# The first batch's pooled remainder in the prologue, and a fourth buffer for raw weights

## The chip, the cores and the metric

One core of one Trainium2 chip runs the whole kernel. The metric is the device time of one execution in microseconds (us). TensorE does the matmuls, VectorE and ScalarE the element work, GpSimd (POOL) additions and indirect DMAs, SyncE (SP) issues the plain DMAs.

## The reference, cut to what matters

Three layers follow one another. The first is attention over 4 batches, 8 heads, 576 positions, 64 wide, and its output is the sum of two attentions: one over sequences pooled by 4 (144 positions, repeated 4 times), one over a local band. The other two are layers of 8 experts, each token going to one.

```python
q_d = q.reshape(B, H, Sd, factor, D).mean(axis=3)      # k_d, v_d alike; Sd = 144
out_up = np.repeat(sm_attn(q_d, k_d, v_d), factor, axis=2)
mask = np.abs(pos[:, None] - pos[None, :]) < factor
scores = np.where(mask, scale * np.matmul(q, k.transpose(0, 1, 3, 2)), -1e9)
...
return out_up + np.matmul(softmax(scores), v)
# _moe_ref, N = 2304, D = 512, E = 8, F = 1024 (the second layer has no output gate)
e_idx = np.argmax(x @ w_gate, axis=1)
h = np.maximum(x[mask] @ w1[e], 0.0)
out[mask] = gate_w[mask, None] * eom[mask, e, None] * (h @ w2[e])
```

## The kernel before, in words

**Pooled attention.** A batch has 144 pooled queries for each head. Heads go in 4 pairs; class `Pooled(b, c)` does the first 128 queries of pair c = 0 to 3, and with c = 4 the *remainder*, the last 16 queries' part of all pairs at once (32 rows a pair, so that four column tiles of TensorE hold four pairs). Its steps: `scores` (matmuls into a bank of PSUM), `smax` (maximum and difference on VectorE), `exps` (ScalarE), `flip` (three transposes on TensorE), `evac` (copy on ScalarE), `pvs` (product with the pooled values `vpd`), `norm`. Pooled sums come from POOL for the most part (`sums_k`, `sums_q`, `sums_v`). In the first batch the pairs 0 and 1 don't wait for pooled queries: their scores are four matmuls, one for each of the four positions that are pooled, that add up in PSUM (`QPE = 2`). For the remainder of that batch (L517 to L528) this makes four matmuls for each of the pairs 0 and 1, one pair after the other, and one each for the pairs 2 and 3; a matmul of f32 is two instructions in the trace.

**Local attention.** `Local(i)` does one of 20 tiles (5 a batch): `scores`, softmax, `flip`, `pvs` (which also adds the pooled output `od` through a 0/1 matrix `rep`), `xevac` (copies rows to SBUF and stores 58 or fewer rows with each of two DMAs, L690), transposes, and the logits of the first expert layer.

**Order.** The prologue is a list of names, `PRO` (L72): `F` sums of keys, `s`, `m`, `f` the start, middle and finish of a pooled pair, `V` and `A` sums, `l...` loads. Then 23 steps follow; each runs `ORDER` over up to three local tiles in different stages and the pooled work set for that step (`pooled_at`). The remainder of the first batch is set for step 0 (`REM0`), so its scores are in step 0 and its transposition and product in step 1. From this order, which gives priorities, a planner in the compiler makes the order on each engine; it goes by its own estimate of when inputs are there, and an instruction of lower priority can pass one that isn't ready. On the chip each engine then works in that fixed order. All pooled work and transposes in attention share a pool of two PSUM buffers (`psx`).

**Experts.** The first layer's tokens are routed as attention goes (`route`: `pick`, `count`, `place`, `spread`, `put`; `put` is a matmul into a list in PSUM). After step 18 the fullest expert so far is picked (`snap`), its first 256 rows are gathered by indirect DMA (`fetch`, L1156), and weights are loaded ahead (`prime`). Weights come in 128 chunks c of 512 KB: `load_next` loads a chunk into one of `NRAW` buffers, `split_next` casts it to its high part `wh` (ScalarE, L1127) and takes the remainder `wl` (VectorE, L1135), which frees the buffer. A job's rows are transposed (`xpose`, L1206) and cast to `xh` (ScalarE, L1216) and `xl` (VectorE, L1219). `hide` makes one of eight hidden blocks with 12 matmuls, two blocks a chunk; chunks 4 to 7 are the second matrix.

**Edges written by hand.** The cast of chunk 0 is put behind the last transposed copy of attention, and the cast of chunk `PINX` behind the casts of the first job's rows:

```python
if c in (0, PINX):
    for p in after if c else front:
        tc.add_manual_dep(i.ins, p.ins.name, ...)   # "the rows go ahead of weights"
i = nc.vector.tensor_tensor(lo, raw, hi.bitcast(F32), op=ALU.subtract)
if c == PINX:
    tc.add_manual_dep(i.ins, placed[0].ins.name, ...)  # "the places of the last tokens go ahead"
```

`PINX` is 4 with three raw buffers, so the chunks 0 to 2 are loaded ahead, chunk 3 is the first to wait for a buffer, and the edge holds chunk 4.

Of the kernel before, what the change touches and what calls it, by code (L numbers as in the profile page):

```python
# [9 lines left out]
F32 = mybir.dt.float32  # L10
# [11 lines left out]
NP = H // 2  # L22
SD = S // 4
# [5 lines left out]
DM = 512  # L29
# [5 lines left out]
MAGIC = 12582912.0  # L35
NOV = 32
NWB = 9
NRAW = 3

CAPS = (  # L40
    (512, 384, 352, 320, 304, 288, 272, 256),
# [6 lines left out]
NWE = 3  # L48
POOLSPLIT = 0
POOLHI = 0  # L50
REM0 = 0
PUTN = 2
PB = (3, 2, 3, 2, 1)
PUTS = 15
# [9 lines left out]
XA = 99  # L64
STEPF = {}
RLATE = 0
PINX = 4
QPE = 2
KPOOL = 0
Q1POOL = 0  # L70
S1 = "pppp"
PRO = "F0 s0 V0 s1 F2 s2 s3 zq m1 Ls m0 m2 f0 f1 lqk lvr f2 m3 V1 A0 lcs rep A2 f3 Le lvw zp lw1"  # L72
ORDER = "R As Ae q0f Cf Xt Cp p0s Xl Xs An p0e q1f p1s q0p Cx D p1e K q1p S"

C_ID = 0
# [105 lines left out]
def moe_pair_kernel(  # L181
# [17 lines left out]
    nc = tc.nc  # L199
# [194 lines left out]
    def attention(actx, early, early_x, front):  # L394
# [11 lines left out]
        kpd = [side[i].tile([128, 2, NP, SD], F32, name=f"kpd{i}") for i in range(2)]  # L406
# [3 lines left out]
        rep = sb1.tile([128, NTP + NP, 128], F32R, name="rep")  # L410
        qd = {}
# [83 lines left out]
        class Pooled:  # L495
# [6 lines left out]
            def scores(self):  # L502
                b, c = self.b, self.c
                ps = psx.tile([128, 512], F32, tag="m", name="s")
                sv = ps[:, 0:2 * SD].rearrange("p (s k) -> p s k", s=2)
                if c < NP:
                    if b == 0 and c < QPE:
                        src = qt[b % 3][:, c, 0:512].rearrange("p (t r) -> p t r", r=4)
                        for r in range(4):
                            nc.tensor.matmul(  # L510
                                sv, lhsT=src[:, :, r], rhs=kpd[b % 2][:, :, c, :],
                                start=(r == 0), stop=(r == 3),
                            )
                    else:
                        nc.tensor.matmul(sv, lhsT=qd[b][:, c, 0:128], rhs=kpd[b % 2][:, :, c, :])
                else:
                    for a in range(NP):  # L517
                        if b == 0 and a < QPE:
                            src = qt[b % 3][:, a, S - 128:S].rearrange("p (t r) -> p t r", r=4)
                            ls = [src[:, :, r] for r in range(4)]  # L520
                        else:
                            ls = [qd[b][:, a, SD - 32:SD]]
                        for i, l in enumerate(ls):
                            nc.tensor.matmul(
                                sv[32 * a:32 * a + 32], lhsT=l,
                                rhs=kpd[b % 2][:, :, a, :], tile_position=(0, 32 * a),
                                start=(i == 0), stop=(i == len(ls) - 1), skip_group_check=True,
                            )  # L528
                self.sv = sv

            def smax(self):
# [189 lines left out]
        pooled_at = {}  # L721
        for b in range(B):
            s0 = NTP * (b - 1) + 2
            for c in range(NP + 1):
                if b or c == NP:
                    pooled_at.setdefault(s0 + c // 2 if b else REM0, []).append(Pooled(b, c))
        groups = GROUPS
        lgs_of = {}
        for g0, gn in groups:
# [29 lines left out]
        for i in range(3):  # L759
            t = sb3.tile([128, 3, 128], F32, tag="p", name="p")  # L760
            nc.sync.dma_start(t, crep[:, 3 * i:3 * i + 3])
            stg.append(t)
        c0 = [Pooled(0, c) for c in range(NP)]

        def start(c):
            c0[c].scores()
# [41 lines left out]
            "A0": lambda: sums1(0),  # L808
            "A2": lambda: sums1(2),
        }  # L810
        for c in range(NP):
            pro.update({
                f"s{c}": lambda c=c: start(c), f"m{c}": lambda c=c: middle(c), f"f{c}": lambda c=c: finish(c),
            })
        for o in PRO.split():
            pro[o]()

        for s in range(-1, NL + 3):
# [6 lines left out]
            if 0 <= s:  # L825
                b, r = s // NTP + 1, s % NTP
# [143 lines left out]
    def experts():  # L970
        pl = {}
# [4 lines left out]
        def pool(nm, bufs=1, **kw):  # L976
            pl[nm] = ctx.enter_context(tc.tile_pool(name=nm, bufs=bufs, reuse_waits="tile", **kw))

        def pools_early():
            pool("raw", NRAW)  # L980
            pool("xr", 5)
            pool("x0")
            pool("w0", NWE)
            pool("h0")
            pool("sm", 2)
# [109 lines left out]
        def load_next():  # L1095
            c = nxt[0]
            if c >= len(stream) or c - nxt[1] >= NRAW:
                return
# [4 lines left out]
            if j == 0:  # L1103
                M.e_sp[r] = M.eid(r)
            raws[c] = pl["raw"].tile([128, 1024], F32, tag="raw", name="raw", bufs=NRAW)
            load_w(raws[c], M, M.e_sp[r], j, M.by_rows[r])
# [43 lines left out]
        def prime():  # L1150
            for _ in range(NRAW):
                load_next()
# [13 lines left out]
        def fetch(job, fresh=None):  # L1166
# [10 lines left out]
            seen = tiles // NTP * S + tiles % NTP * 2 * GQ  # L1177
            x = []
            for k, mm in job.slots:
                xr = pl["xr"].tile([128, DM], F32, tag="xr", name="xr", bufs=5)  # L1180
                gather(M, xr, ri, k, mm, seen if job is M0.jobs[0] else NT)
                x.append(xr)
            job.x = x
# [121 lines left out]
        def overflow_slot(M, m, nov, i):  # L1305
# [39 lines left out]
            nc.vector.scalar_tensor_tensor(  # L1345
                ri[:, 0, 1:2], rf[:, 0, 0:1], -1.0, bg, op0=ALU.add, op1=ALU.add
            )
            xr = pl["xr"].tile([128, DM], F32, tag="xr", name="xr", bufs=5)
            gather(M, xr, ri, 0, 128)
            pt = psx.tile([128, 4, 128], F32, tag="m", name="t")  # L1350
            for d in range(4):
# [5 lines left out]
            for j in range(8):  # L1357
                raw = pl["raw"].tile([128, 1024], F32, tag="raw", name="raw", bufs=NRAW)
                load_w(raw, M, e, j)
                rv = raw.rearrange("p (a w) -> p a w", w=256 if j < 4 else 128)  # L1360
                if j < 4:
                    for f2 in range(2):
                        ph = psx.tile([128, 512], F32, tag="m", name="ph")
                        for d in range(4):
                            nc.tensor.matmul(
                                ph[:, 0:128], lhsT=rv[:, d, 128 * f2:128 * f2 + 128], rhs=xt[:, d],
                                start=(d == 0), stop=(d == 3),
                            )
                        nc.scalar.activation(ht[:, 2 * j + f2], ph[:, 0:128], func=AF.Relu)
                else:  # L1370
                    for f in range(8):
                        nc.tensor.matmul(
                            py[:, 128 * (j - 4):128 * (j - 4) + 128], lhsT=ht[:, f], rhs=rv[:, f],
                            start=(f == 0), stop=(f == 7), skip_group_check=True,
# [259 lines left out]
```

## Time and profile before

| what | value |
|---|---|
| median of 3 runs | 747.93 us (747.17 to 748.26) |
| profiled execution | 742.5 us, its span 740.7 us |
| TensorE busy | 697.6 us, 94% of the span |
| VectorE, ScalarE, POOL busy | 446.3, 343.5, 184.6 us |
| mean granted TensorE clock | 0.972 |

A profile lists the instructions of one execution by engine. PE is TensorE's matmuls, PEld its weight loads, DVE VectorE, ACT ScalarE. `out<-in` are the program's tile names. Behind an instruction, in brackets, is the idle time of its engine just before it and what ended that. The granted clock is a share of 2.4 GHz; 0.50 is 1.2 GHz. Times count from the start of the span.

### The profile page before, as it was taken

The numbers are of one execution on the slowest core, as the hardware profiler recorded it, in microseconds if no ns is written. First come the engines' busy times: TensorE is split into PE (matmuls) and PEld (weight loads), VectorE is DVE, ScalarE is ACT, GpSimd is POOL, SyncE is SP. The second block draws the span as 40 slices with busy tenths as digits, with TensorE's granted clock in tenths as the row PEclk, the third lists the DMA queues.
The fourth block names the chain that finished last, engine by engine and source line by source line (L and its number), as shares of the span: only waits on it lengthen the run. The fifth ranks groups of instructions, "written<-read, shape, count | busy, mean of one in ns | idle before, by whom it ended". The sixth has DMA issues, their size and how long they took to land. (4 is left out here: it accounts for less than half of the span.)

```text
span 740.7 us, 15853 instructions
## 1 busy us (share of the span) xinstructions
PE 697.6 (94%) x6048; PEld 637.4 (86%) x6048; DVE 446.3 (60%) x1160; ACT 343.5 (46%) x634; POOL 184.6 (25%) x227
## 2 busy tenths in 40 slices
PE   8799899976989999999999999989999999999993
PEld 5468677765989999999999999878999999999992
DVE  7486979785667656575766776645444444555520
ACT  4055657584255353545454554155335354554620
POOL 5994720010131203121130130142013030321211
PEclk9699999996999999999999999999999999999998
DMA  9945553143176435445555461366435354565500
GB/s 354 420 140 210 184 196 132 55 156 131 58 247 207 160 121 183 140 161 179 173 176 168 141 221 59 110 213 217 128 111 182 126 186 141 176 193 178 163 21 16
DMA packets 52990, 120.99 MB, mean 163 GB/s; under 512 B 4800, under 2 KB 26176, under 8 KB 51884
## 3 DMA queue, kind: packets, MB, share of 16 engines
q1 hardware_dynamic: 45772, 99.19, 39.9%
q0 software_dynamic: 7136, 20.72, 8.2%
q8 instruction: 50, 0.82, 0.5%
q14 instruction: 32, 0.26, 0.1%
HBM read 101.01 MB, written 20.71 MB: 164 GB/s over the span
## 5 line engine op out<-in xcount | busy, mean ns | idle before, releaser
L1135 DVE TENSOR_TENSOR wl<-raw,wh 128x1024 fp32r<-128x1024 f32 x128 | 156.2, 1224 | 115.7 <-ACT wh L1127 115.4
L1127 ACT CAST wh<-raw 128x1024 fp32r<-128x1024 f32 x128 | 133.2, 1048 | 197.7 <-PE py L1295 113.3
L1294 PE MATMUL ph<-xh,wh 128*128 128x256 f32 (+8 forms) x576 | 172.3, 307 | 6.6 <-ACT xh L1216 6.6
L1295 PE MATMUL ph<-xl,wh 128*128 128x256 f32 (+8 forms) x576 | 175.6, 307 | 0.0
L1296 PE MATMUL ph<-xh,wl 128*128 128x256 f32 (+8 forms) x576 | 174.8, 305 | 0.0
L1294 PE MATMUL py<-h,wh 128*128 128x256 f32 (+8 forms) x448 | 138.4, 316 | 0.0
L1295 PE MATMUL py<-h,wh 128*128 128x256 f32 (+8 forms) x448 | 137.8, 311 | 0.0
L1296 PE MATMUL py<-h,wl 128*128 128x256 f32 (+8 forms) x448 | 137.4, 310 | 0.0
L1294 PEld LDWEIGHTS ph<-xh,wh 128*128 128x128 f32 x576 | 108.1, 190 | 8.4 <-ACT xh L1216 7.2
L1296 PEld LDWEIGHTS ph<-xh,wl 128*128 128x128 f32 x576 | 109.2, 190 | 0.6
L1295 PEld LDWEIGHTS ph<-xl,wh 128*128 128x128 f32 x576 | 109.1, 189 | 0.7
L1421 DVE SCALAR_TENSOR_TENSOR h<-ph,h 128x256 fp32r<-128x256 f32 (+8 forms) x144 | 66.2, 471 | 39.2 <-ACT h L1420 38.7
L1420 ACT ACTIVATE h<-ph 128x256 fp32r<-128x256 f32 (+8 forms) x144 | 60.7, 423 | 56.2 <-PE ph L1296 55.0
L1295 PEld LDWEIGHTS py<-h,wh 128*128 128x128 f32 x448 | 84.1, 188 | 0.6
L1296 PEld LDWEIGHTS py<-h,wl 128*128 128x128 f32 x448 | 84.1, 188 | 0.6
L1294 PEld LDWEIGHTS py<-h,wh 128*128 128x128 f32 x448 | 83.4, 188 | 0.9
L1156 POOL DMA_INDIRECT xr<-x,ri x49 | 50.3, 1026 | 97.1 <-PE t L1206 76.8
L1222 POOL DMA_INDIRECT out<-yr,ri x25 | 25.8, 1032 | 128.6 <-ACT yr L1240 84.2
L1222 POOL DMA_INDIRECT x<-yr,ri x24 | 25.1, 1044 | 126.3 <-ACT yr L1240 118.2
L1216 ACT CAST xh<-t 128x512 fp32r<-128x512 f32 (+5 forms) x49 | 26.1, 533 | 25.6 <-PE t L1206 25.5
L1494 DVE COPY yT<-py 128x256 f32<-128x256 f32 (+8 forms) x28 | 13.7, 490 | 39.9 <-PE py L1296 39.9
L1219 DVE TENSOR_TENSOR xl<-t,xh 128x512 fp32r<-128x512 f32 (+5 forms) x49 | 30.1, 620 | 10.5 <-ACT xh L1216 10.3
(194 smaller groups left out, 1041.8 us busy)
## 6 DMA issues: line engine op xcount, KB each, us to landing
raw<-w_a SPq DMA_DIRECT2D x64, 512.0 KB
raw<-w_b SPq DMA_DIRECT2D x64, 512.0 KB
vraw<-vr SPq DMA_DIRECT2D x4, 1560.0 KB
vd<-vw SPq DMA_DIRECT2D x4, 1280.0 KB
kd<-kT SPq DMA_DIRECT2D x8, 586.0 KB
qt<-qT SPq DMA_DIRECT2D x8, 586.0 KB
x<-zx SPq DMA_DIRECT2D x6, 768.0 KB
x<-x SPq DMA_DIRECT2D x36, 116.0 KB
```

Of the source, the lines that this page charges most:

```text
L1127: i = nc.scalar.copy(hi, raw)
L1135: i = nc.vector.tensor_tensor(lo, raw, hi.bitcast(F32), op=ALU.subtract)
L1156: g = nc.gpsimd.indirect_dma_start(xr[0:mm], None, src, bass.IndirectOffsetOnAxis(ap=ri[0:mm, k, 0:1], axis=0))
L1216: i = nc.scalar.copy(xh[:, :, o], pt[:, :, 0:mm])
L1219: nc.vector.tensor_tensor(xl[:, :, o], pt[:, :, 0:mm], xh[:, :, o].bitcast(F32), op=ALU.subtract)
L1222: i = nc.gpsimd.indirect_dma_start(M.dst[:, :], bass.IndirectOffsetOnAxis(ap=ri[0:mm, k, 1:2], axis=0), yr[0:mm], None, bounds_check=NT - ...
L1294: nc.tensor.matmul(ps, lhsT=ah, rhs=bh, start=first, stop=False)
L1295: nc.tensor.matmul(ps, lhsT=ah, rhs=bl, start=False, stop=False)
L1296: nc.tensor.matmul(ps, lhsT=al, rhs=bh, start=False, stop=last)
L1420: nc.scalar.activation(a[:, 0:n], ph[:, 0:n], func=AF.Relu)
L1421: nc.vector.scalar_tensor_tensor(b_[:, 0:n], ph[:, 0:n], 0.0, a[:, 0:n].bitcast(F32), op0=ALU.max, op1=ALU.subtract)
L1494: nc.vector.tensor_copy(yT[:, dc, 0:n], py[:, 0:n])
```

## The change

The remainder of the first batch is no longer in the steps: `s4`, `m4` and `f4` stand in the prologue's list, behind `m2`, `m3` and `f3`. The remainder's scores are made in turns: the first matmul of each of the four pairs, then the second of each pair that has more, and so on; for the other batches, with one matmul a pair, the order stays. There are four raw buffers instead of three, and four buffers of gathered rows instead of five. The hand-written edges go to chunk 3.

```diff
-NRAW = 3
+NRAW = 4
-REM0 = 0
-PINX = 4
+PINX = 3
-PRO = "F0 s0 V0 s1 F2 s2 s3 zq m1 Ls m0 m2 f0 f1 lqk lvr f2 m3 V1 A0 lcs rep A2 f3 Le lvw zp lw1"
+PRO = "F0 s0 V0 s1 F2 s2 s3 zq m1 Ls m0 m2 s4 f0 f1 lqk lvr f2 m3 m4 V1 A0 lcs rep A2 f3 f4 Le lvw zp lw1"
...
+                    ls = []
                     for a in range(NP):
                         if b == 0 and a < QPE:
                             src = qt[b % 3][:, a, S - 128:S].rearrange("p (t r) -> p t r", r=4)
-                            ls = [src[:, :, r] for r in range(4)]
+                            ls.append([src[:, :, r] for r in range(4)])
                         else:
-                            ls = [qd[b][:, a, SD - 32:SD]]
-                        for i, l in enumerate(ls):
-                            nc.tensor.matmul(
-                                sv[32 * a:32 * a + 32], lhsT=l,
-                                rhs=kpd[b % 2][:, :, a, :], tile_position=(0, 32 * a),
-                                start=(i == 0), stop=(i == len(ls) - 1), skip_group_check=True,
-                            )
+                            ls.append([qd[b][:, a, SD - 32:SD]])
+                    for i in range(4):
+                        for a in range(NP):
+                            if i < len(ls[a]):
+                                nc.tensor.matmul(
+                                    sv[32 * a:32 * a + 32], lhsT=ls[a][i],
+                                    rhs=kpd[b % 2][:, :, a, :], tile_position=(0, 32 * a),
+                                    start=(i == 0), stop=(i == len(ls[a]) - 1), skip_group_check=True,
+                                )
...
-                if b or c == NP:
-                    pooled_at.setdefault(s0 + c // 2 if b else REM0, []).append(Pooled(b, c))
+                if b:
+                    pooled_at.setdefault(s0 + c // 2, []).append(Pooled(b, c))
...
-        c0 = [Pooled(0, c) for c in range(NP)]
+        c0 = [Pooled(0, c) for c in range(NP + 1)]
...
-            pool("xr", 5)
+            pool("xr", 4)
```

## Rows read from the trace of the kernel before

**Rows 1.** The page: busy time by engine, and the clock in 40 slices.

```profile
PE 697.6 (94%) x6048; PEld 637.4 (86%) x6048; DVE 446.3 (60%) x1160; ACT 343.5 (46%) x634; POOL 184.6 (25%) x227
...
PEclk9699999996999999999999999999999999999998
```

**Rows 2.** Windows by stage: stretch and its length, then busy time by engine, clock, DMA.

```profile
160.00:184.00 24.00, 13.11 (x118) 10.55 (x118) 15.68 (x76) 13.50 (x28) 2.66 (x5) 0.64 0.42 138
...
240.00:480.00 240.00, 240.00 (x1769) 231.29 (x1768) 157.01 (x456) 109.97 (x186) 44.82 (x58) 1.00 0.46 153
```

**Rows 3.** TensorE's waits in 160 to 192: total us, times, longest.

```profile
PE ph L1294 <- ACT xh L1216: 5.9, 1, 5.9
```

**Rows 4.** Timeline of ScalarE at the handover: start us, duration us.

```profile
163.28 2.94 ACT L1127 CAST wh<-raw 128x1024 fp32r<-128x1024 f32 x3
...
168.82 0.59 ACT L1216 CAST xh<-t 128x512 fp32r<-128x512 f32 x1 [2.43 <-PE t L1206]
174.60 1.04 ACT L1127 CAST wh<-raw 128x1024 fp32r<-128x1024 f32 x1 [5.20 <-DMA raw<-w_a]
175.56 0.58 ACT L1216 CAST xh<-t 128x512 fp32r<-128x512 f32 x1
```

**Rows 5.** Timeline of SP's queue: the weight loads.

```profile
153.25 1.55 SPq L1088 DMA_DIRECT2D raw<-w_a  x3
...
165.61 0.37 SPq L1088 DMA_DIRECT2D raw<-w_a  x1
```

**Rows 6.** Timeline of TensorE at the handover.

```profile
169.15 1.11 PE L1206 MATMUL t<-ident,xr 128*128 128x128 f32 x4 [0.37 <-DMA xr<-x,ri]
...
176.19 1.44 PE L1294 MATMUL ph<-xh,wh 128*128 128x256 f32 x5 [5.92 <-ACT xh L1216]
...
191.11 0.28 PE L1294 MATMUL py<-h,wh 128*128 128x256 f32 x1
```

**Rows 7.** Windows at the handover: columns as in rows 2.

```profile
168.00:172.00 4.00, 1.89 (x8) 1.09 (x6) 2.03 (x12) 0.59 (x1) 0.00 (x0) 0.50 0.94 301
172.00:176.00 4.00, 0.00 (x0) 0.00 (x0) 0.32 (x1) 1.40 (x2) 0.00 (x0) 0.50 0.18 74
176.00:180.00 4.00, 3.43 (x13) 2.96 (x14) 3.93 (x17) 4.00 (x11) 0.00 (x0) 0.50 0.43 142
180.00:184.00 4.00, 4.00 (x34) 3.76 (x34) 2.06 (x16) 2.28 (x6) 0.00 (x0) 0.94 0.00 0
```

**Rows 8.** Timeline of TensorE in the prologue and the first steps.

```profile
16.91 0.52 PE L550 MATMUL t<-ident,pd 128*128 128x128 f32 x3 [0.38 <-ACT pts L554]
19.18 0.71 PE L564 MATMUL v<-vpd,pts 128*128 128x130 f32 x4 [1.75 <-POOL vpd L488]
...
27.28 0.87 PE L550 MATMUL t<-ident,pd 128*128 128x128 f32 x3 [0.58 <-DVE od L589]
28.78 1.67 PE L564 MATMUL v<-vpd,pts 128*128 128x130 f32 x6 [0.62 <-ACT pts L554]
30.38 3.99 PE L524 MATMUL s<-kpd,qt 128*32 128x288 f32 x13
...
35.03 0.39 PE L659 MATMUL v<-odh,rep 128*128 128x256 f32 x1
...
38.03 0.87 PE L570 MATMUL v<-vpd,pts 128*32 128x130 f32 x24
...
55.72 1.06 PE L564 MATMUL v<-vpd,pts 128*128 128x130 f32 x8
```

**Rows 9.** Timeline of VectorE: the last tokens' places, then weight remainders.

```profile
185.47 0.16 DVE L326 TENSOR_TENSOR key<-key,cs 128x2 f32<-128x2 f32 x1
...
185.74 3.49 DVE L1135 TENSOR_TENSOR wl<-raw,wh 128x1024 fp32r<-128x1024 f32 x3
```

**Rows 10.** TensorE's waits for gathered rows in the whole run.

```profile
PE t L1206 <- DMA xr<-x,ri: 3.0, 4, 1.8
```

**Rows 11.** Timeline of POOL: the second batch's pooled values.

```profile
49.61 5.20 POOL L488 TENSOR_TENSOR vpd<-vraw 64x260 f32<-64x260 f32 x6
```

More of the change, by code (lines that the diff above doesn't have):

```diff
@@ L810, in attention @@
         }
-        for c in range(NP):
+        for c in range(NP + 1):
             pro.update({
@@ L1179, in fetch @@
             for k, mm in job.slots:
-                xr = pl["xr"].tile([128, DM], F32, tag="xr", name="xr", bufs=5)
+                xr = pl["xr"].tile([128, DM], F32, tag="xr", name="xr", bufs=4)
                 gather(M, xr, ri, k, mm, seen if job is M0.jobs[0] else NT)
@@ L1347, in overflow_slot @@
             )
-            xr = pl["xr"].tile([128, DM], F32, tag="xr", name="xr", bufs=5)
+            xr = pl["xr"].tile([128, DM], F32, tag="xr", name="xr", bufs=4)
             gather(M, xr, ri, 0, 128)
```

## The prediction

> **What bounds the kernel now.** I read the share of busy time first, then the busy time by stage, then the waits of TensorE, and last the two places where it waits longest, instruction by instruction. TensorE is busy 94% of the span, and two of forty slices show its clock well under full: the second, in the prologue, and the tenth [rows 1]. The table by stage shows that this 94% is two different things: in the expert stage between 240 and 480 us TensorE has no idle time at all at full clock, while the 24 us in which attention hands over to the experts have 13.11 us of work at a mean clock of 0.64 [rows 2]. An edit that only feeds the expert stage faster can thus win nothing; what can be won lies at the handover and in the prologue. The longest single wait at the handover is one of 5.9 us: the first expert matmul waits for a cast of gathered rows on ScalarE [rows 3].
>
> ScalarE shows why. It casts three weight chunks, then the first 128 gathered rows at 168.82, and then has nothing else in its queue than the cast of the fourth chunk (c=3), for which it waits 5.20 us; the second 128 rows are cast only behind it, at 175.56 [rows 4]. Three chunks were loaded ahead at 153.25; the fourth had to wait for a free buffer and was issued at 165.61 [rows 5]. The rows themselves were ready long before: their transposes ran from 169.15 for 1.11 us, so they ended at 170.26. TensorE starts at 176.19 [rows 6]. The clock is at half (1.2 GHz) all through 168 to 180, and back in the stretch 180 to 184 [rows 7]. The other place is the prologue: TensorE waits for the pooled values (1.75 us in one go), and from 30.38 to 35.03 it does nothing but the remainder's scores, at half clock for most of it, with the first tile's product behind them [rows 8].
>
> **The change part by part.** *Fourth raw buffer and pin on the fourth cast.* Now four chunks are loaded ahead, so the chunk that ScalarE waited for is there before the rows, and its cast is put behind both casts of rows by an explicit edge. The second cast of rows can then start when the transposes end: 170.26, cast 0.58 [rows 4], first matmul at about 170.95 with the gap of 0.05 that it has today. Against 176.19 that is 5.24 us. The first six hidden blocks need chunks 0 to 2, which are cast by 166.22 [rows 4]. What is late next? The remainder of chunk 3 is pinned behind the places of the last tokens, which in the rows end at 185.63, with three chunk remainders in 3.49 behind [rows 9]. So one remainder is ready at about 185.8 + 1.2 = 187.0, 10.8 us after TensorE's start, and moves with the routing chain, since VectorE stood behind the same cast. Eight blocks took from 176.19 to 191.11 [rows 6], 14.9 us, 2.1 of which half clock cost (next paragraph); (14.9 - 2.1) / 8 = 1.6 us a block at full clock, so block 6 begins 3.2 us before 191.11, 11.7 us after the start. The cover is 0.9 us; without it a remainder's length, 1.2, is lost. I take 0, bounds 0 and +1.2.
>
> Half clock: from 176.19 to about 180.4 the matmuls ran at half speed (the stretch 180 to 184 has a mean of 0.94, so 0.5 for its first 0.5 us) [rows 7]; that cost 2.1 us. If full clock returned with the first matmul it would be -2.1; if it only returned at the same hour, 9.4 us would run at half, +2.6. I take the same 4.2 us, 0, as the nearest row.
>
> The fourth load ahead: one more 512 KB. At the 301 GB/s of the stretch 168 to 172 [rows 7] it is 1.7 us of transfer, issued behind the other three at 153.25 [rows 5] on SP's queue; behind it there stand the row stores of the last tiles, and the gathers share the engines. The gathers gate the transposes, so the cost lies between 0 and 1.7; I take 0.5, nearer to 0 since the loads are issued 12 us before it matters. Four buffers for gathered rows instead of five: TensorE's waits for gathered rows are 3.0 us in the whole run [rows 10], and gathers are issued a job ahead; I take 0, bounds 0 and +1. In the expert stage the deeper prefetch meets a TensorE with no idle time: 0, bounds 0 and +0.5 for a transfer that now comes earlier beside others.
>
> *The remainder in the prologue.* It leaves: the scores' block, 35.03 - 30.38 = 4.65 us, a transposition (0.52 at full clock) and the product, 0.87 for 24 matmuls [rows 8]. It comes in: the scores right behind the third transposition at 17.43, where the trace has a wait of 1.75 and then more waits for the pooled values. In turns, the two columns of eight instructions run beside each other and not after each other, so about half of 4.65, 2.3 us at the old clocks, and less at full clock: it fills the 1.75 and runs over by 0.6 at most, which the next wait hides. Its transposition (0.87 at half clock, as the one at 27.28) and its product (0.87 at full clock, 1.74 at half) come around the fourth pair's product, which ends at 30.45. With both before the first tile, that begins at 30.45 + 0.87 + 1.74 = 33.06, against 35.03: -2.0. With the transposition and product that no longer lie in the first two steps (0.52 + 0.87) the best is -3.4. But attention is not free to run earlier: the second batch's products (8 matmuls at 55.72) follow POOL's pooled values, 49.61 + 5.20 = 54.81 [rows 8, 11], and POOL's queue doesn't get shorter. From there at most 55.72 - 54.81 = 0.9 is left, unless the planner fills in other work. I take -1.0; bounds -3.4 and, if the planner's new order costs what the old one saved, +1.0. The exponentials and maxima of the remainder are the same instructions on VectorE and ScalarE, moved: 0. The memory for the remainder's own scores is in a pool of two buffers; it is why the bound above is not better.
>
> **Sum.** -5.24 + 0 + 0.5 for the handover, -1.0 for the front: -5.7 us. The profiled execution took 742.5 us (span 740.7), and would take 736.8; the median of the runs shown is 747.93, 5.4 above it. The difference carries over, so the forecast is 747.93 - 5.7 = 742.2 us.
>
> **Rivals.** *A, the wait goes on behind the rows.* Both casts of rows run, but the next thing in ScalarE's queue is the fifth chunk (c=4), which is not loaded ahead and which no edge holds back. ScalarE keeps its order, as [rows 4] show, and behind that cast there stand the list matrices that TensorE's queue has after its first five matmuls. Then TensorE does those 1.44 us [rows 6] and stops until the chunk lands, as late as the fourth did. Gain 1.44 + 1.0: 745.5 us. For it: nothing in the code holds c=4 back. Against: the list matrices belong to earlier steps of the program, and go first where their inputs are there.
>
> *B, the fifth chunk takes the fourth's place, and it is slower.* The first chunk that isn't loaded ahead was put between the two casts of rows by the planner, because by its own reckoning it had landed. That chunk is now c=4; its load is issued when the first remainder is done, as before, and the edge has moved to c=3. If its cast stands there again, ScalarE waits again, and for longer by one more chunk on the way: 1.7. With the front's gain given back at POOL it is 747.93 + 1.7 = 749.6 us. It decides if this cast stands ahead of the second rows and its transfer lands after 170.26. For it: the load issued at 165.61 was waited for until 174.60, 9 us, though from 172 on the DMA share was 0.18 [rows 4, 5, 7]: a part of the transfer comes late, and a fifth load would meet that too. Against: the place between the two casts is about a microsecond wide, and the order is planned afresh.
>
> By the Trainium skill (page DMA: Bandwidth & Descriptors, section Why a DMA increments its semaphore by 16 and not by 1) a DMA uses the largest number of engines up to 16 that divides the slowest dimension on both sides; a store of 58 rows would use two. By that rule the tiles' stores fill two engines, and each chunk's share there queues behind them. The trace agrees as far as it goes, a late landing at a DMA share of 0.18, and it would make B's landing certain, and only the cast's place open.
>
> *C, the same place but the front's gain stays.* As B, the longer wait eaten by the front: 747.93 + 1.7 - 1.0 = 748.6, and 746.2 with the whole 3.4 of it; I take 747.5 between them. It is also what I'd see if the edit's pin did nothing.
>
> **Chances.** Forecast 0.44 (its own range 739.5 to 745), A 0.19 (744 to 747), C 0.17, B 0.20 (748.5 to 751). The two new orders by the planner put 1 to 2 us on each. A measurement of this kernel can tell some 0.2%, 1.5 us: faster is below 746.4, slower above 749.4. Faster: 0.43 + 0.11 + 0.04 = 0.58. Slower: 0.18 from B, 0.03 from the others' upper ends: 0.21. Within: 0.21. The range goes from 739.5, the forecast with half of the front's and clock's better bounds, to 750.0, which holds B's centre; about one in ten lies outside on each side.
>
> **What would show it.** Right: on ScalarE both casts of rows before the fourth chunk's; the 5.9 us wait for the rows' cast gone; the first expert matmul 0.8 us behind the second transposes, near 170 on the scale of before. In the prologue: remainder scores between 17 and 21 us, 20 instructions in about 2 us, and the first tile's product 1 to 3 us earlier. Wrong: a chunk's cast with a DMA wait of some microseconds ahead of the second rows (B, C) or of the list matrices with TensorE idle behind its first five matmuls (A); block 6 waiting for a remainder; the second batch's products no earlier than 55.7 (front lost); a clock that comes back later than 4.2 us after the start.

## The result, and the profile after

The changed kernel takes 752.74 us (median of 5 runs, 750.41 to 754.02) where the kernel before took 747.17 beside it (5 runs): a ratio of 1.0076, 95% interval 1.0059 to 1.0094, 5.6 us slower. The forecast was 742.2 us, range 739.5 to 750.0, so the prediction was wrong in its sign. The profiled executions are 742.5 (span 740.7) and 750.41 us (span 748.6); the second is the fastest of its five.

The prologue, on TensorE, in the form of [rows 8]:

```profile
17.59 0.47 PE L526 MATMUL s<-kpd,qt 128*32 128x288 f32 x2
17.61 0.68 PE L526 MATMUL s<-kpd,qd 128*32 128x288 f32 x4
17.89 1.87 PE L526 MATMUL s<-kpd,qt 128*32 128x288 f32 x14
...
32.30 0.37 PE L661 MATMUL v<-odh,rep 128*128 128x256 f32 x1
...
55.05 0.78 PE L566 MATMUL v<-vpd,pts 128*128 128x130 f32 x2
...
56.27 2.37 PE L566 MATMUL v<-vpd,pts 128*128 128x130 f32 x10
```

The remainder's 20 instructions take 2.2 us where the wait for the pooled values was, and the first tile's product comes 2.7 us earlier than in [rows 8] (32.30 against 35.03). By the second batch's products all of that is gone: they follow POOL, whose pooled values end at 55.14 us (54.81 before), and now run at half clock (0.50 from 54 to 58 us, where the kernel before has 1.00).

At the handover, TensorE's waits in 160 to 192, to be held against [rows 3]:

```profile
PE list L361 <- ACT bm L352: 1.2, 2, 0.6
...
PE ph L1296 <- ACT xh L1218: 0.7, 1, 0.7
```

and ScalarE's timeline, against [rows 4]:

```profile
171.24 0.58 ACT L1218 CAST xh<-t 128x512 fp32r<-128x512 f32 x1 [2.21 <-PE t L1208]
172.88 0.58 ACT L1218 CAST xh<-t 128x512 fp32r<-128x512 f32 x1 [1.05 <-PE t L1208]
173.36 1.05 ACT L1129 CAST wh<-raw 128x1024 fp32r<-128x1024 f32 x1
178.53 1.05 ACT L1129 CAST wh<-raw 128x1024 fp32r<-128x1024 f32 x1 [4.11 <-DMA raw<-w_a]
179.48 0.71 ACT L352 ACTIVATE bm<-oc,v 128x144 fp32r<-128x144 f32 x2
```

Both casts of rows now go ahead and the 5.9 us wait is 0.7. But ScalarE then stands 4.11 us in front of the fifth chunk's cast, with the list matrices (bm) behind it. This is the wait of the prediction's rival A, though TensorE doesn't stop behind its first five matmuls: it has others, and waits for the list only from 179.6 us on. What the wait costs is seen 20 us later, in TensorE's timeline from the last logits of attention (lT) to the first transposition back (t<-ident,yT):

```profile
169.08 0.61 PE L716 MATMUL lT<-cs,lts 128*128 128x16 f32 x2 [1.84 <-ACT lts L709]
...
173.52 1.44 PE L1296 MATMUL ph<-xh,wh 128*128 128x256 f32 x5 [0.68 <-ACT xh L1218]
...
180.25 0.46 PE L361 MATMUL list<-bm,am 128*128 128x432 f32 x1 [0.65 <-ACT bm L352]
...
204.88 0.66 PE L1208 MATMUL t<-ident,xr 128*128 128x128 f32 x4 [0.98 <-DMA xr<-x,ri]
...
208.08 1.08 PE L381 MATMUL lT<-yT,wg 128*32 128x256 f32 x8 [2.54 <-DVEq L1304]
...
212.04 1.05 PE L1240 MATMUL t<-ident,yT 128*128 128x128 f32 x4
```

The same places of the kernel before:

```profile
166.44 0.60 PE L714 MATMUL lT<-cs,lts 128*128 128x16 f32 x2 [1.61 <-ACT lts L707]
...
206.06 0.64 PE L382 MATMUL lT<-yT,wg 128*32 128x256 f32 x8 [1.97 <-DVEq L1302]
...
208.25 0.60 PE L1238 MATMUL t<-ident,yT 128*128 128x128 f32 x4
```

With the first expert matmul at 176.19 before [rows 6], three marks cut each profile into four pieces: the last logits of attention (166.44, 169.08), the first expert matmul (176.19, 173.52), the first transposition back (208.25, 212.04) and the end (740.7, 748.6). The change costs 2.6 us up to the end of attention, wins 5.3 up to the first expert matmul (9.75 to 4.44 us), loses 6.5 in the first job (32.06 to 38.52), and 4.1 in the rest (532.45 to 536.56): 7.9 together. The first job loses by waits for the list (1.2, against 0.4 before), for hidden values (h, 0.6) and for the second job's rows (0.98), by 0.57 more in front of the logits behind the job (L381), by 0.7 at its start, where half clock lasts longer, and by 1.8 in a stretch at half clock that was not there before: from those logits to the transposition back it now takes 3.96 us (208.08 to 212.04), and 2.19 before. These are some 5.5 of the 6.5 us. The stretch shows in the windows of the changed kernel (columns as in [rows 2]):

```profile
204.00:208.00 4.00, 0.66 (x4) 0.42 (x4) 1.38 (x2) 1.11 (x2) 0.05 (x1) 0.80 0.05 13
208.00:212.00 4.00, 3.92 (x21) 3.11 (x22) 0.55 (x6) 0.37 (x1) 2.57 (x5) 0.50 0.76 228
```

### The profile page after: what moved, and what is told of

Read it like the earlier page. It is cut to its first block, busy times and chain, and to the rows that moved or that the text cites. A ratio compares the mean times of both kernels' runs of the same rounds, so it can differ in the third digit from the quotient of the medians.

```text
span 748.6 us, 15846 instructions
## 1 busy us (share of the span) xinstructions
PE 702.7 (94%) x6048; PEld 644.0 (86%) x6048; DVE 446.2 (60%) x1160; ACT 342.8 (46%) x634; POOL 183.9 (25%) x227
## 5 line engine op out<-in xcount | busy, mean ns | idle before, releaser
L1297 PE MATMUL ph<-xl,wh 128*128 128x256 f32 (+8 forms) x576 | 177.4, 310 | 0.0
L1296 PE MATMUL ph<-xh,wh 128*128 128x256 f32 (+8 forms) x576 | 174.4, 311 | 1.4 <-ACT xh L1218 0.7
L1296 PEld LDWEIGHTS ph<-xh,wh 128*128 128x128 f32 x576 | 110.3, 194 | 3.8 <-issue 1.9
L1297 PEld LDWEIGHTS ph<-xl,wh 128*128 128x128 f32 x576 | 111.1, 193 | 0.6
L1298 PEld LDWEIGHTS ph<-xh,wl 128*128 128x128 f32 x576 | 111.0, 193 | 0.6
L1158 POOL DMA_INDIRECT xr<-x,ri x49 | 52.5, 1071 | 138.7 <-PE t L1208 109.2
```

The costliest lines, as they stand in the source:

```text
L1158: g = nc.gpsimd.indirect_dma_start(xr[0:mm], None, src, bass.IndirectOffsetOnAxis(ap=ri[0:mm, k, 0:1], axis=0))
L1296: nc.tensor.matmul(ps, lhsT=ah, rhs=bh, start=first, stop=False)
L1297: nc.tensor.matmul(ps, lhsT=ah, rhs=bl, start=False, stop=False)
L1298: nc.tensor.matmul(ps, lhsT=al, rhs=bh, start=False, stop=last)
```

## The experiments

All ratios are to the kernel before, run on the same chip in turns. **Theory 1**: the prologue loses at POOL's values, the handover gives its gain back at the list. The **rivals**: all is lost at one of the two; or the loss lies in the buffers of rows.

**The two parts by themselves.** One run has only the remainder in the prologue (with its turns), one only `NRAW = 4`, `PINX = 3` and four row buffers.

> The kernel before with only the remainder moved to the prologue and its scores in turns; three raw buffers, the edges on chunk 4 and five buffers of gathered rows as before. Theory 1 (the front's gain is lost behind POOL's values of the second batch and overturned by two new stretches at half clock): the last tile's x copy 2 to 3 us later than before, and the time 2 to 3 us above before. Rival 1 (the prologue's 2.7 us carry through, and the whole loss is made at and behind the handover): 1 to 3 us below before. Rival 2 (the front's change doesn't reach the end of attention at all): within 0.5 us of before.

> The kernel before with only four raw buffers, four buffers of gathered rows and the edges on chunk 3; the remainder stays in the steps. Theory 1 (first expert matmul 5.2 us earlier, but the fifth chunk's cast stands ahead of the last list matrices on ScalarE and the gain is given back at the second job, and some 3.5 us more are lost at the first job of the second layer): 2 to 4 us above before. Rival 1 (the handover's gain is kept and the loss came with the prologue): 4 to 5 us below before. Rival 2 (given back, but nothing lost later): within 1 us of before.

Measured: the prologue alone 1.0032 (1.0018 to 1.0046), the handover alone 1.0033 (1.0015 to 1.0052). Each part loses 2.4 to 2.5 us, and together they make up most of the change's 5.6. Theory 1's times hold, and no part carries the loss alone; what the prologue's part loses is shown further down to lie near 85 us, not at the second batch's values. The pieces of the profile say the same: the handover alone goes from the last logits to the first expert matmul in 3.97 us and then takes 39.24 for the first job; the prologue alone has 9.77 and 32.47, as before, but ends attention at 171.21.

**The list ahead of the fifth chunk.**

```diff
+                if c == PINX + 1:    # behind ScalarE's last copy of a list matrix
+                    tc.add_manual_dep(i.ins, bmc[0].ins.name, ...)
```

> The changed kernel with one more edge: the cast of the fifth chunk (c=4) goes behind ScalarE's last copy for the last tokens' list. Theory 1 (this cast, waiting 4.1 us for its transfer, held the list and with it the gathers of the second job): the list's matmuls no longer wait, the second job's gathers come 3 to 5 us earlier, and the time is 4 to 6 us below the changed kernel, 0 to 2 us above before. Rival 1 (the list is late for another reason, the attention that ends 2.6 us later): 0 to 1 us below the changed kernel. Rival 2 (the chunks 4 to 7 are then late for the second matrix, and TensorE waits there): no gain or 1 to 2 us above the changed kernel.

Measured: 0.9972 (0.9955 to 0.9990), which is 0.0104 or 7.8 us below the changed kernel, more than expected. ScalarE's timeline with the edge:

```profile
173.67 1.05 ACT L1130 CAST wh<-raw 128x1024 fp32r<-128x1024 f32 x1
174.62 1.32 ACT L353 ACTIVATE bm<-oc,v 128x144 fp32r<-128x144 f32 x4
...
185.28 2.93 ACT L1130 CAST wh<-raw 128x1024 fp32r<-128x1024 f32 x3
```

POOL's first gather of the second job with the edge:

```profile
192.94 1.14 POOL L1165 DMA_INDIRECT xr<-x,ri  x1 [1.39 <-issue]
```

and in the changed kernel:

```profile
199.82 0.97 POOL L1158 DMA_INDIRECT xr<-x,ri  x1 [1.40 <-issue]
```

It comes 6.9 us earlier, TensorE's waits for the list are gone, and the first job takes 32.14 us instead of 38.52, while the first expert matmul still starts 4.42 us behind the last logits. The list was the reason; the chunks moved behind it were not missed. The handover's part alone with this edge:

> The handover's part alone (four raw buffers, edges on chunk 3, the remainder in the steps as before) with the edge that puts the fifth chunk's cast behind the list's last copy. Theory 1 (the two parts of the change add up, and the prologue's costs 2.4 us in either company): 2 to 3 us below the run with the prologue (743.7), 741 to 742, that is 4 to 5.5 us below before. Rival 1 (with the list ahead the front's hour no longer matters, since something later sets the end): 743 to 744.5.

Measured: 0.9920 (0.9906 to 0.9935), some 6 us below before, a little more than expected. The pieces are 3.90 and 31.70 us.

**Four buffers of rows**, alone (`xr` 5 to 4 in the kernel before):

> The kernel before with four buffers of gathered rows instead of five, all else as before. Theory 1 (the fifth buffer lets the second layer's first gathers be issued ahead; without it TensorE waits some 1 to 2 us longer there, and the clock falls to half behind the wait): 2 to 4 us above before, all of it between 480 and 520 us. Rival 1 (those waits come from the deeper weight prefetch, or from the handover's new hour, not from the row buffers): within 0.5 us of before.

Measured: 0.9995 (0.9980 to 1.0010). Theory 1's share for it is refuted; the forecast's 0 was right. Yet this profile has two stretches at half clock, near 208 and 488 us (0.69 from 208 to 212, 0.50 from 488 to 492), that the first profile of before lacks, which asked for a second profile of before:

> The kernel before, once more, for a second profile of it. Theory (the first profiled execution of before, 742.5 us against a median of 746.25, had fewer stretches at half clock than is usual, and so the 7.9 us between the two profiles overstate the change by 2 us): this profile has one or two stretches at half clock more, near 205 and near 488 us, and a span of 743 to 746 us. Rival (such stretches belong to the changed kernel alone): no stretch at half clock between 185 and 730 us, span 740 to 742.

Measured: span 742.2 us, no such stretch. Neither answer fits whole: the span is 1.5 us above the first, without half clock after 185 us. So the first profile was a short one, and the 7.9 us between the profiles overstate the 5.6 of the medians; the stretches can't be counted from one profile each. The changed kernel with both edges (below), profiled twice, showed a stretch near 200 us once and not the other time.

**POOL beside VectorE.** Why attention ends later is seen near 85 us. First POOL's timeline in the kernel before:

```profile
68.10 4.33 POOL L485 TENSOR_TENSOR vraw<-vraw 128x520 f32<-128x520 f32 x3 [10.46 <-DMA vraw<-vr]
...
83.61 0.67 POOL L481 TENSOR_TENSOR qd<-tm 128x288 f32<-128x288 f32 x1
87.43 3.80 POOL L485 TENSOR_TENSOR vraw<-vraw 128x520 f32<-128x520 f32 x3 [3.15 <-DMA vraw<-vr]
```

and VectorE's there, the places of the first tiles, a chain of small instructions that the list matrices wait for:

```profile
84.81 0.15 DVE L323 SCALAR_TENSOR_TENSOR pp<-kk,jj 128x5 f32<-128x5 f32 x1
...
85.03 0.47 DVE L349 TENSOR_SCALAR am<-cs,pp 128x128 fp32r<-128x128 f32 x2
...
85.61 0.50 DVE L350 TENSOR_SCALAR oc<-cs,key 128x144 f32<-128x144 f32 x2
```

POOL in the changed kernel:

```profile
62.17 3.78 POOL L484 TENSOR_TENSOR vraw<-vraw 128x520 f32<-128x520 f32 x3 [4.65 <-DMA vraw<-vr]
...
83.12 3.77 POOL L484 TENSOR_TENSOR vraw<-vraw 128x520 f32<-128x520 f32 x3 [5.39 <-DMA vraw<-vr]
```

and VectorE in it:

```profile
82.88 0.68 DVE L641 TENSOR_REDUCE sm<-p 128x8 f32<-128x512 f32 x1
83.48 0.95 DVE L322 SCALAR_TENSOR_TENSOR pp<-kk,jj 128x5 f32<-128x5 f32 x1
...
85.60 2.06 DVE L348 TENSOR_SCALAR am<-cs,pp 128x128 fp32r<-128x128 f32 x2
...
87.77 0.91 DVE L349 TENSOR_SCALAR oc<-cs,key 128x144 f32<-128x144 f32 x2
```

Before, this part of VectorE's chain ran in a gap of POOL's (84.3 to 87.4). Now POOL's adds for the third batch start at 62.17 us, not 68.10, so the load behind them goes out earlier (at 73.27 on SP's queue, not 79.79), and the last batch's adds fall on the chain: `pp` takes 0.95 us instead of 0.15, the two `am` masks 2.06 instead of 0.47. The third batch's values come earlier though their load goes out at the same hour (55.16, before 54.83): the loads of keys and queries that stood right ahead of it on SP's queue (48.04 to 52.80) now go out at 42.13 to 44.15, and the DMA share from 50 to 56 us is 0.13 to 0.15 instead of 0.92 to 1.02. That this is why it lands sooner is read from the two traces, not tested.

By the Trainium skill (page SBUF — State Buffer, section Who interferes with whom) VectorE and GpSimd share a pair of SBUF ports, held for a whole instruction; instructions with two inputs from SBUF, and masks of this kind (`tensor_scalar`) in a mode that uses both of VectorE's port pairs, can wait for it, while reductions don't. The trace agrees: the reduction at 82.88 takes 0.68 us though POOL's add begins in it (83.12), and 0.68 in the next run, where POOL is idle.

The test holds these adds behind the chain. Their call moves three steps back in the program with it, and the order of instructions on POOL and VectorE stays what it was:

```diff
 i = eng.tensor_tensor(vraw[:, k, 0:2], vraw[:, k, 0:2], vraw[:, k, 2:4], op=ALU.add)
+if b == 3:
+    tc.add_manual_dep(i.ins, ocs[1].ins.name, ...)    # a wait for VectorE's second oc
...
-if r == (1 if s > 4 else 2):
+if r == (4 if s > 4 else 2):
     sums_v(b + 1)
```

> The changed kernel with the list's edge, and POOL's adds for the last batch's pooled values wait for VectorE's second position mask (oc) of the first group of tiles; every engine's order is the same. Theory 1 (the front loses at POOL's adds: they come 4 us earlier than before, and run beside VectorE's chain of small instructions for the places, which take 2 to 4 times as long beside them): VectorE's two am masks back from 2.1 us to 0.5, TensorE's wait for the list from 4.4 to about 2 us, the last tile's x copy 2 to 2.5 us earlier, the time 2 to 2.5 us below the run without the wait (743.7). Rival 1 (the chain is slow for another reason, such as the half clock before it): VectorE's times as without the wait, no gain. Rival 2 (the later adds make a later product wait): the chain is faster, but TensorE waits 2 us more for the last batch's values, no gain.

Measured: 0.9884 (0.9869 to 0.9899), 738.12 us. POOL with this wait:

```profile
84.87 4.17 POOL L486 TENSOR_TENSOR vraw<-vraw 128x520 f32<-128x520 f32 x3 [7.13 <-DVE oc L351]
```

and VectorE:

```profile
83.49 0.15 DVE L324 SCALAR_TENSOR_TENSOR pp<-kk,jj 128x5 f32<-128x5 f32 x1
...
83.70 0.48 DVE L350 TENSOR_SCALAR am<-cs,pp 128x128 fp32r<-128x128 f32 x2
...
84.29 0.50 DVE L351 TENSOR_SCALAR oc<-cs,key 128x144 f32<-128x144 f32 x2
```

The masks are back at 0.48 us. TensorE's first wait for the list there, in the kernel before, in the changed one and with both edges:

```profile
87.02 0.47 PE L362 MATMUL list<-bm,am 128*128 128x432 f32 x1 [3.15 <-ACT bm L353]
...
89.58 0.73 PE L361 MATMUL list<-bm,am 128*128 128x432 f32 x1 [4.43 <-ACT bm L352]
...
85.70 0.47 PE L363 MATMUL list<-bm,am 128*128 128x432 f32 x1 [0.54 <-ACT bm L354]
```

With the list's edge alone it is 4.8 us. The last logits come at 164.15 instead of 169.41 with that edge alone. Starting POOL's adds 1.75 us later (84.87 against 83.12 in the changed kernel) thus brings 5.3 us there, twice what was expected, and 0.0088 or 6.6 us of the time; the half clock from 87 to 94 us (0.50 from 88 to 92) goes with it. Three more runs say whose doing the collision is.

> The prologue's part alone (as the run that gave 749.05) with POOL's adds for the last batch behind the places of the first tiles. Theory 1 (the whole loss of that part, and more, is the collision of POOL and VectorE near 85 us): 743 to 745.5, 1 to 3.5 us below before. Rival 1 (the part loses also elsewhere, at the new half clock near 52 us): the collision goes, but the time stays within 1 us of before.

> The changed kernel with only POOL's adds behind the places of the first tiles, the fifth chunk's cast ahead of the list as it was. Theory 1 (the two losses add up: 5 us at POOL, the rest at the list): 4 to 6 us below the changed kernel, that is within 1.5 us of before. Rival 1 (the end of attention isn't what sets the end while the list is late): less than 2 us below the changed kernel, 3.5 us or more above before.

> The kernel before, with POOL's adds for the last batch behind the places of the first tiles, and nothing else; every engine's order is the same. Theory 1 (before, these adds start at 87.4 us, behind the mask that the edge names, so the edge holds nothing; the collision came with the prologue's part): within 0.7 us of before. Rival 1 (the edge is worth 4 to 5 us to any of these kernels, and the loss of the prologue's part has nothing to do with the edge's gain): 3 us or more below before.

Measured: the prologue alone with the edge 0.9936 (0.9915 to 0.9956), the whole change with it 0.9995 (0.9984 to 1.0006), the kernel before with it 1.0001 (0.9983 to 1.0020). The edge is worth nothing to the kernel before, where the adds start at 87.77 anyway, and some 6 to 7 us to each kernel with the prologue's part (0.0096, 0.0081, 0.0088). As the call moved there too, the move by itself is worth nothing. The two losses add up: from 1.0076, POOL's edge takes 0.0081 and the list's 0.0104, and both together 0.0192 (0.0170 in a second run, below).

One run was to show that the second batch's values hold the front near 55 us, by taking a sum off POOL (`S1 = "pppd"`):

> The changed kernel with both edges, and the sum of pooled queries of pairs 2 and 3 of the second batch on VectorE and not on POOL. Theory 1 (POOL's queue up to the second batch's pooled values, 55.1 us, is what eats the prologue's gain): with some 1.9 us less in it (1.2 for the first add, 0.67 for the second) the values end near 53 us, the fourth tile's x copy comes 1 to 2 us earlier, and the time is 1 to 2 us below 738.1. Rival 1 (VectorE is full in these steps, and the sum on it delays the softmax of tiles 2 to 4 by as much): the values end earlier, the x copies don't, the time within 1 us of 738.1 or above it.

Measured: 0.9920 (0.9897 to 0.9943). It tells nothing: the new order put another add ahead, and the values ended at 55.6 us all the same. That the front loses there stays read from the trace, not shown.

**The second layer.** In 470 to 500 us kernels with four raw buffers wait longer for the second gather of the second job (1.2 to 1.8 us in most, 0.7 to 0.9 in three, against 0.24 before).

> The changed kernel with the list's edge, and with only three chunks loaded ahead for the second layer's first expert. Theory 1 (the fifth load, issued between the second layer's first two gathers and behind four others, delays the second gather; with three ahead there is one load less in the engines' way): TensorE's second wait for gathered rows, 1.2 to 1.7 us with four buffers, falls to 0.2 to 0.4; the time 1 to 2 us below the run without it (743.7). Rival 1 (that gather is late since it is issued late relative to the last products): the wait stays above 1 us, and the time within 0.7 us of that run.

> The changed kernel with both edges (list ahead of the fifth chunk, POOL behind the places), and for the second layer's first expert each load waits until the remainder three chunks earlier is taken, as three raw buffers would make it; holding them by the program's order alone left four loads ahead. Theory 1 (the fourth and fifth load crowd the gathers of that job): TensorE's second wait for gathered rows, 0.7 us in the run without it, falls to 0.2 to 0.4, the time 0.5 to 1.5 us below 738.1. Rival 1 (the second gather is late for another reason): the wait stays at 0.7 or more, the time within 0.5 us. Rival 2 (a chunk that is loaded later is missing at the job's second matrix): TensorE waits there, 1 to 2 us slower.

> The changed kernel with both edges, and one of the four raw buffers passed over once at the start of the second layer, so that the fourth load of its first expert waits for the first chunk's remainder, as with three buffers. Theory 1 (four loads at once crowd the gathers behind them): the fourth load is issued some 4 us later, TensorE's second wait for gathered rows there falls from 0.7 to 0.4 or less, the first from 2.2 to 1.9, and the time is 0.5 to 1.5 us below 738.1. Rival 1 (the gathers' own chain, not the loads, makes that wait): the load is later, the waits are not shorter, time within 0.5 us.

Measured: 0.9960, 0.9898 and 0.9893, no different from the same kernels without the hold. These three held the wrong chunks, those of the second layer's first expert. SP's queue in the last of them shows that these come from 415 us on; the loads beside the gathers belong to the second expert:

```profile
415.58 9.08 SPq L1098 DMA_DIRECT2D raw<-w_b  x4
...
468.66 2.06 SPq L1098 DMA_DIRECT2D raw<-w_b  x4
474.48 0.69 SPq L1103 DMA_DIRECT2D raw<-w_b  x1
```

So the same hold, by a small write into the buffer behind an earlier remainder, went to the second expert's fourth load, with the kernel of both edges beside it, and then to its fifth:

```diff
-            if c >= len(stream) or c - nxt[1] >= NRAW:
+            if c >= len(stream) or c - nxt[1] >= NRAW - (72 <= c < 80):
...
+            if c == 75:      # in the second of the two: c == 76, behind los[73]
+                k = nc.vector.memset(raws[c][:, 0:1], 0.0)
+                tc.add_manual_dep(k.ins, los[72].ins.name, ...)
```

> The changed kernel with both edges, and the fourth load of the second layer's second expert (c=75) held until its first chunk's remainder is taken. The earlier runs that were to hold a load held the first expert's, which had come 50 us before; the loads beside the gathers near 475 us are the second expert's. Theory 1 (four loads at once, and a fifth between the gathers, crowd them): TensorE's second wait for gathered rows near 478 us falls to 0.4 or less, the first to 1.9, and the time is 0.5 to 2 us below the same kernel without the hold in this call. Rival 1 (the gathers' own chain makes that wait): the load is later, the wait stays at 0.7 to 1.7, time within 0.5 us.

> The changed kernel with both edges once more, beside the run with the held load and for a second profile of it: 737 to 740 us, 7 to 9 us below before, the second wait for gathered rows at 0.7 to 1.7.

> The changed kernel with both edges, and of the second layer's second expert four loads go ahead as they do, while the fifth (c=76, the first of its second matrix, in pieces of 512 bytes) is held until the second chunk's remainder is taken, as with three buffers. So far the second wait for gathered rows grew with what was issued between the two gathers: 0.2 us with one chunk of the first matrix (before), 1.7 with one of the second matrix (both edges), 2.8 with one of each (the held load). Theory 1 (the second matrix's chunk with its many small pieces, issued between the gathers, delays the second): the wait falls to 0.5 or less, and the time is 1 to 2 us below the run with both edges (738.3). Rival 1 (four loads at once are enough to delay it): the wait stays above 1 us, the time within 0.7 us. Rival 2 (the chunk held is missed later): TensorE waits at that expert's second matrix.

Measured: both edges 0.9906 (0.9892 to 0.9919), 738.29 us; the fourth load held 0.9915 (0.9901 to 0.9928); the fifth held 0.9867 (0.9837 to 0.9896), 736.79 us, the lowest median of all. TensorE's transposes of that job with both edges:

```profile
476.30 0.66 PE L1222 MATMUL t<-ident,xr 128*128 128x128 f32 x4 [2.07 <-DMA xr<-x,ri]
478.63 1.11 PE L1222 MATMUL t<-ident,xr 128*128 128x128 f32 x4 [1.67 <-DMA xr<-x,ri]
```

with the fourth load held:

```profile
476.42 0.81 PE L1230 MATMUL t<-ident,xr 128*128 128x128 f32 x4 [2.03 <-DMA xr<-x,ri]
480.00 1.11 PE L1230 MATMUL t<-ident,xr 128*128 128x128 f32 x4 [2.77 <-DMA xr<-x,ri]
```

with the fifth held:

```profile
477.12 0.66 PE L1230 MATMUL t<-ident,xr 128*128 128x128 f32 x4 [1.51 <-DMA xr<-x,ri]
478.47 1.12 PE L1230 MATMUL t<-ident,xr 128*128 128x128 f32 x4 [0.70 <-DMA xr<-x,ri]
```

Holding the fourth load sent the fifth out right behind it (472.37 and 472.95 us, the gathers at 471.56 and 473.41), and the second gather came later still. Without the fifth chunk between the gathers both waits shrink, 3.7 to 2.2 us, the second to 0.7, not below 0.5 as expected. The first profile of both edges has 0.74 for the second wait without the hold, so the waits alone don't settle it. The time from the second gather's issue to the transposes of its rows does better: it is 4.9 to 5.5 us in ten of the eleven profiles in which the fifth chunk was issued alone between the two gathers, 6.7 in the eleventh, and 3.6 to 3.8 in both profiles of before and with the fifth held.

So a chunk of the second matrix between two gathers goes with a later second gather, and four loads ahead don't by themselves. That the hold wins time is not shown: its interval overlaps those of both runs of both edges (0.9884 and 0.9906), and the profiled executions of the hold and of both edges beside the fourth load have the same span, 736.4 us.

## Why the prediction was wrong

- **Second cast of rows, -5.24**: right. From the last logits to the first expert matmul it is 5.3 us less.
- **Rival A set at 0.19**: here the prediction failed. Its reason against A, that the list matrices "belong to earlier steps of the program, and go first where their inputs are there", didn't hold. The order is made before the run, from estimates, and it put the fifth chunk's cast first; on the chip the list's masks (oc) were done at 172.95 us, and waited behind a cast that waited for its transfer. A's price was wrong too: a gain of 1.44 + 1.0, with TensorE's stall as the only loss. The stall was only 1.2 us, but the list also feeds the second job's gathers, and the first job lost 6.5 us. The trace of before already spoke against the reason given: there the masks were done at 170.53, and the list matrices came at 176.03, behind the fourth chunk's cast; it cost little, as TensorE waited for the rows behind the same cast.

```profile
170.04 0.49 DVE L350 TENSOR_SCALAR oc<-cs,key 128x144 f32<-128x144 f32 x2
...
176.03 0.72 ACT L353 ACTIVATE bm<-oc,v 128x144 fp32r<-128x144 f32 x2
```

- **Front, -1.0, bounds -3.4 and +1.0**: failed. The prediction followed POOL only to 54.81 us, and took "POOL's queue doesn't get shorter" as the end of the matter. The queue moved: third batch's adds 5.9 us earlier, last batch's 4.3, onto VectorE's chain. Measured alone it is +2.4 us, beyond the bound; with POOL's adds held it is -4.8, beyond the other bound. POOL is then idle while VectorE's whole chain runs, and TensorE's wait for the list there is 0.5 us; in the kernel before, the first half of the chain ran beside POOL, and the wait is 3.15.
- **Fourth load ahead, 0.5, and the pinned remainder, 0**: of the right size. No run has these terms alone. With the handover's part alone attention ended 0.8 us later in one run and 0.5 earlier in the other, and with the list ahead the first job takes no longer than before.
- **Four row buffers, 0**: right (0.9995).
- **Expert stage, at most +0.5**: too small, as far as the waits tell. The deeper prefetch meets a TensorE with no idle time between 240 and 480 us, as [rows 2] say, but not in the second layer's second job, where gathers stand on the path: its two waits for rows are 3.8 us in the changed kernel, and 2.05 before. What that is worth in time stays open.
- **Handover's clock, 0**: within its bounds. Half clock lasts from 173.52 to 179.1 us, 5.6 against the 4.2 assumed, 0.7 us lost.
- **The range's lower end**: it takes half of the front's whole -3.4, though -1.0 of it is in the forecast already; by its own rule it is 740.0, not 739.5. This changes nothing here.

With the two edges the change does what was forecast, and more: 0.9884 and 0.9906 in two runs, -7 to -8.7 us, against the -5.7 of the sum. In part that is luck, since the front then gives several times what was forecast for it; with the list's edge alone, which only puts the order as the prediction thought it, it is 0.9972, -2.1 us.

## What to carry to other kernels

When a wait on an in-order engine is removed by moving what waited, the next instruction that waits for a transfer takes its place: ask what stands behind it there, and follow that to its last reader, not to the first stall. Look whether the rows of before show the same order already. A stage that gets earlier sends off its next loads earlier; follow each engine off the path to its next two pieces of work, and see whom they now run beside. One wait added at the right place can be worth more than the wait removed.

## What was not expected of the hardware

- Beside POOL's adds VectorE's small instructions take 2 to 6 times as long (0.15 to 0.95 us, 0.47 to 2.06); the trace of before had this too, in the same chain, where a 128x40 product took 1.06 us at 81.16 us beside POOL and 0.20 in the changed kernel with POOL idle.
- A chunk of the second matrix issued between two gathers goes with a second gather that is 1 to 2 us later. From its issue to TensorE's transposes of its rows it is 3.8 us with nothing between (474.63 to 478.47), 3.7 with a chunk of the first matrix (before, 481.51 to 485.19), 5.4 with one of the second (473.26 to 478.63), 6.6 with one of each (473.41 to 480.00).
- Stretches at half clock come and go between profiles of one kernel: both edges had one near 200 us in the second profile (0.75 in 196 to 200) and none in the first.
